# Attention followed by a mixer MLP: one more block of the first channel product computed with seven small products, and its order of issue written anew

## The chip, the cores and the metric

The kernel runs on one core of one Trainium2 chip. The time is device microseconds of that core for one execution; of the kernel before it is the median of three runs. A profile of one execution, with each engine's instructions in order of time, goes with it.

## What is computed

Inputs are q, k, v (4 batches, 8 heads, 768 rows, 64 columns), 16 centroids per head and four weights. First an attention whose mask lets a query see the keys of its own cluster; the heads side by side give x. Then a mixer on x, all in float32:

```python
# x: (4, 768, 512), from attention
h = np.maximum(x.transpose(0, 2, 1) @ w_tok1, 0.0) @ w_tok2      # 768 -> 256 -> 768, over tokens
u = x + h.transpose(0, 2, 1)
h2 = np.maximum(u @ w_ch1, 0.0) @ w_ch2                          # 512 -> 1536 -> 512, over channels
return (u + h2).astype(np.float32)
```

## The kernel before

**Stages.** Attention goes through 16 pairs of heads (to about 316 us of the profile). Then the token products of batches 0, 1 and 2, 3 (`tok1`, `tok2_chunks`), which add h onto x, so that x becomes u. Then the channel products, batch by batch in the order 0, 2, 3, 1. Each batch has three parts: a part computes 512 of the 1536 hidden columns (`ch1_pair`, the first channel product, with relu) and multiplies them at once with their rows of the second weight (`ch2_chunks`), adding onto x. Twelve parts in all, some 35 us each. After a batch's third part its rows go out.

**Seven products.** A product of two matrices that are cut into 2 x 2 blocks is computed with seven block products in place of eight (Winograd's form): left sums S1 to S4, right sums T1 to T4, and seven products, called by `SEVEN` (L551) `p1` A11 B11, `p5` S1 T1, `c11` A12 B21, `u2` S2 T2, `c12` S4 B22, `c22` S3 T3, `c21` A22 T4. `by_turns` (L746) goes through the 21 chunk products of a second-channel stage in the order p1, p5, c11, u2, c12, c22, c12, c11, c21 and lets VectorE add each bank of PSUM onto x.

The first channel product is such a product too, with 128-column chunks i = 0, 1. In the first part of the first batch all seven are plain (`ch1_plain`, L831). In the other eleven parts (`ch1_sets`, L864) four of the seven block products are themselves computed with seven small ones of 192 columns: Y = A12 B21, P = S1 T1, Z = S4 B22, X = A22 T4. The three others, A11 B11, S2 T2 and S3 T3, are big products of 384 columns, two halves for each chunk. The small ones' own sums of weights are in `w1ss` (`set_lefts`, L602), those of u in `uTss` (`set_rights`, L620).

The results gather in SBUF: a11, p5, c12, a22, a12 (each two chunks of 384 columns). ScalarE copies or relus, VectorE adds a bank of PSUM onto them. a11, c12, a22 and a12 after their relu, and the sums S1 to S4 made of them, are the left side of the second-channel stage.

**Order of the work.** The kernel is issued by hand: each engine runs its instructions in the order of the calls in the program, and waits on semaphores for what they read or overwrite. Three lists hold work to be put between products:

- `late`: what of the first channel product is issued behind the start of the second-channel stage. `between` (L740) takes one entry from it each time. `by_turns` calls it after each chunk product, behind the hook `after[m]` of that step (L765 to L767). Before, `late_1` and `late_2` (L945, L950) are taken after steps 0 and 1.
- `others`: sums of weights and of u for the next stages, on VectorE. One is taken at each `between`.
- `turning`: the transposes of u of the next batch (`u_steps`, L713). `u_take` (L693) copies a block of x into `urows` on ScalarE and issues a DMA transpose into `ucols`; `u_put` (L706) copies `ucols` into uT on ScalarE. Three `u_take` go into the first channel product of a batch's third part (`beside`), the rest, eight `u_put` and five `u_take`, are issued by the hook `after[3]` of the second-channel stage.

In the third part `after[15]` and `after[17]` begin the sums of the next batch's u; the rest are issued between the two batches and through `others`.

**Memory.** x of batch 1 is written to a DRAM tile after the first pair's token products and read back when batch 0 is out, into batch 0's place (L1157, L1215).

Of the kernel before, what the change touches and what calls it, by code (L numbers as in the profile page):

```python
# [18 lines left out]
C = 16  # L19
# [31 lines left out]
def kernel(  # L51
# [49 lines left out]
    tokpool = pool("tokpool", 1, tokens)  # L101
    staging = fast.enter_context(ExitStack())
# [30 lines left out]
    spill = spilled.tile([P, NJ, DM], F32, name="spill")  # L133
    xs = [(x1pool if b == 1 else xpool).tile([P, NJ, DM], F32, name=f"x{b}") for b in range(B)]
# [466 lines left out]

    def set_lefts():  # L602
        if "l2" not in pools:
            pools["l2"] = pools["w2sums"].tile([P, 4, 3, HS], F32, name="w1ss")
        l2 = pools["l2"]
        yx = W["ch1"].rearrange("p f (i r c) -> p f i r c", i=2, r=2)[:, 2:4]
        pz = pools["w1s"][:, 0:3:2].rearrange("p i f (r c) -> p f i r c", r=2)
        for n, both in enumerate((yx, pz)):
            blocks = [both[:, f, :, r] for r in range(2) for f in range(2)]
            sums_ = [l2[:, 2 * n : 2 * n + 2, m] for m in range(3)]  # L610
            yield dict(
                zip(("A11", "A12", "A21", "A22", "S1", "S2", "S4", "S3"), blocks + sums_ + blocks[2:3])
            )
# [6 lines left out]
    def set_rights():  # L620
        uT, R, r2 = pools["uT"], pools["R"], pools["r2"]
        yz = uT[:, :, 2:4].rearrange("p n f (k t) -> p n f k t", k=2)
        x, p = (R[name].rearrange("p f (k t) -> p f k t", k=2) for name in ("T4", "T1"))
        for blocks, sums_ in (
            ([yz[:, :, f, k] for f in range(2) for k in range(2)], [r2[:, 0:2, m] for m in range(3)]),
            ([x[:, f, k] for f in range(2) for k in range(2)], [r2[:, 2, m] for m in range(3)]),
            ([p[:, f, k] for f in range(2) for k in range(2)], [r2[:, 3, m] for m in range(3)]),
        ):
            yield dict(
                zip(("B11", "B12", "B21", "B22", "T1", "T2", "T4", "T3"), blocks + sums_ + blocks[1:2])  # L630
            )

    def set_right_sums():

        pools["r2"] = pools["w2sums"].tile([P, 4, 3, HS // 2], F32, name="uTss")
        return [list(winograd_right(blocks)) for blocks in set_rights()]

    def set_blocks():

        (yx, pz), (yz, x, p) = (list(y) for y in (set_lefts(), set_rights()))  # L640
        left = {name: {k: a[:, i] for k, a in two.items()} for two, i, name in
                ((yx, 0, "Y"), (yx, 1, "X"), (pz, 0, "P"), (pz, 1, "Z"))}
        right = {"Y": {k: b[:, 0] for k, b in yz.items()}, "Z": {k: b[:, 1] for k, b in yz.items()},
                 "X": x, "P": p}
        return left, right
# [100 lines left out]
    def by_turns(n, product, of, last=False, after=()):  # L746
# [10 lines left out]
        for m in range(len(order) // 2):  # L757
# [9 lines left out]
            between()  # L767
# [16 lines left out]
    def ch1_pair(part, sets, beside):  # L784
# [6 lines left out]
        p5, c12 = (pools["mlp"].tile([P, 2, HS], F32, name=k) for k in ("p5", "c12"))  # L791
# [10 lines left out]

        def big(psum, a, r, i, start):
            product(psum, a, r, i, start)
            between()
            if a != "A11" and beside:
                beside.pop(0)()
# [13 lines left out]
        def sums_34():  # L821
            nc.vector.scalar_tensor_tensor(
                out=h2["S3"], in0=c12, scalar=0.0, in1=a11, op0=ALU.max, op1=ALU.subtract
            )
            sub(h2["S4"], a12, h2["S2"])

        (ch1_sets if sets else ch1_plain)(
            part, product, big, relu, a11, a12, a22, p5, c12, sum_1, sum_2, sums_34
        )

    def ch1_plain(part, product, big, relu, a11, a12, a22, p5, c12, sum_1, sum_2, sums_34):  # L831
# [24 lines left out]
        def late_(i):  # L856
            product(X[i], "A22", "T4", i, False)
            nc.scalar.activation(out=a12[:, i], in_=X[i], func=ACT.Relu)
            (sums_34 if i else sum_2)()
# [4 lines left out]
    def ch1_sets(part, product, big, relu, a11, a12, a22, p5, c12, sum_1, sum_2, sums_34):  # L864

        left, right = set_blocks()
        n0, n1 = slice(0, HS // 2), slice(HS // 2, HS)

# [7 lines left out]
        def direct(bank, which, start=True):  # L876
            small(bank[:, n0], which, "c11", start)
            small(bank[:, n1], which, "c12", start)

        def chain(q, which, name, x):  # L880

            small(q[:, n0], which, name, name == "p1")
            src = q[:, n0]
            if len(x.shape) == 3:
                src = src.unsqueeze(1).to_broadcast([P, 2, HS // 2])
            add(x, src, x)

        def column(z, which, x):
            small(z[:, n0], which, "p5")
            add(x[:, :, n1], z[:, n0].unsqueeze(1).to_broadcast([P, 2, HS // 2]), x[:, :, n1])  # L890

        X = [ptile("X", HS), None]
        big(X[0], "A11", "B11", 0, True)
        nc.scalar.copy(out=a11[:, 0], in_=X[0])  # L894
        ybe = ptile("Y", HS)
        direct(ybe, "Y")
        add(a11[:, 0], ybe, a11[:, 0])
        X[1] = ptile("X", HS)
        big(X[1], "A11", "B11", 1, True)
        nc.scalar.copy(out=a11[:, 1], in_=X[1])  # L900
        pbe = ptile("Z", HS)
        direct(pbe, "P")
        nc.scalar.copy(out=p5[:, 0], in_=pbe)
        yq, pq = ptile("Y", HS), ptile("Z", HS)
        chain(yq, "Y", "p1", a11[:, 0, n0])
        chain(pq, "P", "p1", p5[:, 0, n0])
        big(X[0], "S2", "T2", 0, False)
        chain(yq, "Y", "u2", a11[:, 0, n1])
        yz, pz = ptile("X", HS), ptile("Z", HS)
        column(yz, "Y", a11)  # L910
        chain(pq, "P", "u2", p5[:, 0, n1])
        small(pz[:, n0], "P", "p5")
        nc.scalar.copy(out=p5[:, 1, n1], in_=pz[:, n0])
        relu(a11[:, 0])
        add(p5[:, 0, n1], pz[:, n0], p5[:, 0, n1])
        add(c12[:, 0], X[0], p5[:, 0])
        big(X[1], "S2", "T2", 1, False)
        chain(yq, "Y", "c22", a11[:, 1, n1])
        chain(pq, "P", "c22", p5[:, 1, n1])
        direct(ybe, "Z")  # L920
        chain(yq, "Y", "c21", a11[:, 1, n0])
        small(pq[:, n0], "P", "c21", False)
        nc.scalar.copy(out=p5[:, 1, n0], in_=pq[:, n0])
        relu(a11[:, 1])
        add(c12[:, 0], ybe, c12[:, 0])
        chain(yz, "Z", "p1", c12[:, 0, n0])
        add(c12[:, 1], X[1], p5[:, 1])
        big(X[0], "S3", "T3", 0, False)
        add(a22[:, 0], X[0], p5[:, 0])
        relu(a22[:, 0])  # L930
        chain(yz, "Z", "u2", c12[:, 0, n1])
        column(pbe, "Z", c12)
        big(X[1], "S3", "T3", 1, False)
        add(a22[:, 1], X[1], p5[:, 1])
        relu(a22[:, 1])
        chain(yz, "Z", "c22", c12[:, 1, n1])
        direct(X[0], "X", False)
        nc.scalar.copy(out=a12[:, 0], in_=X[0])
        small(X[1][:, n0], "X", "c21", False)
        nc.scalar.copy(out=a12[:, 1], in_=X[1])  # L940
        chain(yz, "Z", "c21", c12[:, 1, n0])
        chain(yq, "X", "p1", a12[:, 0, n0])
        sum_1()

        def late_1():  # L945
            chain(yq, "X", "u2", a12[:, 0, n1])
            column(pz, "X", a12)
            sum_2()

        def late_2():  # L950
            chain(yq, "X", "c22", a12[:, 1].rearrange("p (k t) -> p k t", k=2))
            relu(a12)
            sums_34()

        late.extend([late_1, late_2])
# [166 lines left out]
    for b in (0, 2):  # L1122
# [26 lines left out]
        if b == 2:  # L1149
            take(turning, len(turning))  # L1150
            usums = u_sums()
            tok2_chunks(b, {13: lambda: next(usums)})
        else:
# [3 lines left out]
            nc.sync.dma_start(spill, xs[1])  # L1157
# [7 lines left out]
    batches = (0, 2, 3, 1)  # L1165
    for n, b in enumerate(batches):
        turning = []
        for part in range(3):
# [8 lines left out]
            ch1_pair(part, not first, [turning.pop(0) for _ in turning[:UCOLS]])  # L1177
# [25 lines left out]
            if part == 2 and not last:  # L1203

                yz, x, p = steps
                yz[0]()
                yz[1]()
                next(usums)

                others += [lambda: next(usums)] * 2  # L1210
                others.append(lambda: [step() for step in (yz[2], p[2], yz[3], p[3])])
                others += [lambda: None, lambda: (x[0](), x[1]()), lambda: (x[2](), x[3]())]
                if n == 0:
                    xs[1] = xpool.tile([P, NJ, DM], F32, name="x0")
                    nc.sync.dma_start(xs[1], spill)  # L1215
# [216 lines left out]
```

## Time and profile before

| | us |
|---|---|
| median of 3 runs | 823.48 (823.17 to 823.51) |
| the profiled execution | 823.35 |
| its span, first to last instruction | 821.6 |
| TensorE matmul busy | 814.2, 4348 instructions |
| VectorE busy | 631.1, 1206 instructions |
| ScalarE busy | 374.7, 573 instructions |
| one channel part, 535.7 to 570.7: TensorE, VectorE, ScalarE busy | 35.0, 21.7, 5.6 |

A profile page gives for each engine its busy time (PE is TensorE's matmuls, PEld its weight loads, DVE VectorE, ACT ScalarE, POOL GpSimd, SP the engine that issues DMAs). A line of the order of time reads: start in us, duration in us, engine, line of the program, operation, tile written <- tiles read, shapes, count; in square brackets how long the engine was idle before, and what released it. A float32 product appears as two matmul instructions on TensorE. Instructions overlap a little: the duration of one runs on past the start of the next, so the step from start to start is what a queue of them costs.

The rows of a table of stretches read: stretch, length, busy time and count of PE, PEld, DVE, ACT and POOL, mean granted TensorE clock, DMA share, GB/s.

### The profile page before, as it was taken

What the parts mean: (1) busy time and instruction counts of PE and PEld (TensorE: products, weight loads), DVE (VectorE), ACT (ScalarE), POOL (GpSimd) and SP (SyncE); (2) the same over time, 40 slices, a digit from 0 to 9 for tenths busy, and PEclk for the clock granted to TensorE, in tenths of its full rate; (3) what the DMA queues carried; (4) which work ended last, traced back from release to release, by engine and by line L of the source; (5) the groups of instructions that cost most, each with busy time, mean ns of one, the idle gap of its engine ahead of it and who ended that gap; (6) DMA issues with size and microseconds to landing.
All of it is one profiled execution on the core that took longest, in us unless ns stands there. A gap on an engine that the chain in (4) does not pass through costs nothing.

```text
span 821.6 us, 11693 instructions
## 1 busy us (share of the span) xinstructions
PE 814.2 (99%) x4348; PEld 535.5 (65%) x4348; DVE 631.1 (77%) x1206; ACT 374.7 (46%) x573; POOL 30.7 (4%) x28
## 2 busy tenths in 40 slices
PE   8999999999999999999999999999999999999997
PEld 4444444444444444444588888888888888888876
DVE  6879898989898978859797788755777566775665
ACT  5588776777878776127202154121441204511120
POOL 1001010111011000000000000000000000000000
PEclk9999999999999999999999999999999999999999
DMA  8797666768676434143000025000240001400002
GB/s 156 142 162 135 140 142 122 149 139 163 130 160 137 95 104 122 51 127 79 0 1 1 5 45 183 1 0 1 38 117 0 1 1 30 125 1 1 1 0 81
DMA packets 184258, 63.41 MB, mean 77 GB/s; under 512 B 172800, under 2 KB 176896, under 8 KB 183936
## 3 DMA queue, kind: packets, MB, share of 16 engines
q1 hardware_dynamic: 182592, 62.18, 34.7%
q8 instruction: 36, 0.59, 0.3%
q10 hardware_dynamic: 1600, 0.39, 0.2%
q14 instruction: 30, 0.25, 0.1%
HBM read 36.21 MB, written 7.86 MB: 54 GB/s over the span
## 4 chain that ended last, share of the span: by engine, by line
PE 98%; DVE 1%; issue 0%; ACT 0%; DVEq 0%; ACTq 0%
PE sc L413 19%; PE av L455 15%; PE pX L966 15%; PE pX L798 12%; PE pZ L966 7%; PE ph L534 5%; PE pY L871 5%; PE pZ L871 4%; PE pX L871 4%; PE pY L966 4%; PE pX L774 3%; PE small L491 2%; PE pZ L774 1%; PE small L304 1%; PE pZ L798 1%; PE pY L774 1%
## 5 line engine op out<-in xcount | busy, mean ns | idle before, releaser
L437 ACT ACTIVATE ex<-sc 128x768 f32<-128x768 f32 x192 | 151.0, 812 | 27.2 <-PE sc L413 15.5
L413 PE MATMUL sc<-qkT 64*128 64x384 f32 x768 | 155.3, 483 | 0.0
L445 DVE TENSOR_TENSOR sum<-sum,ex 128x768 f32<-128x768 f32 x128 | 127.8, 999 | 27.1 <-ACT ex L437 14.9
L455 PE MATMUL av<-ex,va 128*64 128x384 f32 x768 | 127.4, 488 | 0.0
L566 DVE TENSOR_TENSOR x<-pX,x 128x256 f32<-128x256 f32 (+1 forms) x168 | 75.8, 458 | 38.1 <-PE pX L966 37.6
L455 PEld LDWEIGHTS av<-ex,va 128*64 128x64 f32 x768 | 53.7, 137 | 71.7 <-issue 67.6
L413 PEld LDWEIGHTS sc<-qkT 64*128 64x128 f32 x768 | 67.8, 187 | 38.3 <-issue 38.0
L810 ACT ACTIVATE hA<-hA 128x384 f32<-128x384 f32 (+1 forms) x57 | 34.0, 597 | 85.4 <-DVE hA L566 85.1
L566 DVE TENSOR_TENSOR hA<-pY,hA 128x192 f32<-128x192 f32 (+1 forms) x90 | 36.7, 407 | 45.4 <-PE pY L871 42.7
L798 PE MATMUL pX<-uT,wc 128*128 128x384 f32 x192 | 69.8, 487 | 0.0
L894 ACT COPY hA<-pX 128x384 f32<-128x384 f32 x11 | 5.3, 479 | 131.3 <-PE pX L798 131.3
L413 PE MATMUL sc<-ohT 64*128 64x384 bf16 x384 | 62.4, 323 | 0.0
L462 ACT COPY avrows<-av 128x768 uint16<-128x768 uint16 x32 | 25.5, 797 | 44.4 <-PE av L455 44.4
L566 DVE TENSOR_TENSOR x<-pZ,x 128x256 f32<-128x256 f32 (+1 forms) x84 | 36.4, 455 | 11.4 <-PE pZ L966 11.3
L798 PEld LDWEIGHTS pX<-uT,wc 128*128 128x128 f32 x192 | 35.4, 190 | 14.7 <-issue 0.6
L534 PE MATMUL ph<-x,wt 128*128 128x512 f32 x96 | 41.6, 593 | 0.0
L413 PEld LDWEIGHTS <-ohT 64*128 64x128 bf16 x384 | 18.7, 94 | 33.8 <-issue 9.6
L966 PE MATMUL pX<-wc,hA 128*128 128x256 f32 x144 | 36.9, 380 | 0.3 <-ACT hA L940 0.3
L711 ACT COPY uT<-ucols 128x768 uint16<-128x768 uint16 x32 | 33.2, 1049 | 4.7 <-DMA ucols<-urows 4.7
L966 PE MATMUL pZ<-wc,hS 128*128 128x256 f32 x144 | 35.0, 379 | 0.0
L966 PE MATMUL pY<-wc,hA 128*128 128x256 f32 x144 | 35.0, 379 | 0.0
L798 PE MATMUL pX<-uTs,w1s 128*128 128x384 f32 x96 | 34.9, 486 | 0.0
(189 smaller groups left out, 1310.8 us busy)
## 6 DMA issues: line engine op xcount, KB each, us to landing
raw<-in_moe_w_ch_dram SPq DMA_DIRECT2D x24, 512.0 KB, 4.5
va<-in_v_dram SPq DMA_DIRECT2D x16, 384.0 KB, 3.7
out_dram<-x SPq DMA_DIRECT2D x24, 256.0 KB, 2.3
qk<-in_k_dram SPq DMA_DIRECT2D x60, 96.0 KB, 4.0
qk<-in_q_dram SPq DMA_DIRECT2D x60, 96.0 KB, 3.5
raw<-in_moe_w_tok_dram SPq DMA_DIRECT2D x3, 512.0 KB, 4.1
raw<-in_moe_w_tok_dram SPq DMA_DIRECT2D x4, 384.0 KB, 3.8
spill<-x SPq DMA_DIRECT2D x1, 1536.0 KB, 5.1
```

Of the source, the lines that this page charges most:

```text
L413: nc.tensor.matmul(sc[:, h, 0:HS], lhsT=src[rows, 1, j], rhs=src[rows, 0, HJ * qh : HJ * qh + HJ], start=start, stop=not start,)
L437: nc.scalar.activation(out=ex, in_=sc[:, :, 0:HS], func=ACT.Exp, scale=SM_SCALE)
L445: nc.vector.tensor_tensor(out=acc, in0=acc if j > 1 else st["ex", qh, 0], in1=st["ex", qh, j], op=ALU.add)
L455: nc.tensor.matmul(av[h * D : (h + 1) * D], lhsT=st["va"][:, h, j], rhs=ex[:, h], start=(j == 0), stop=(j == NJ - 1),)
L534: nc.tensor.matmul(pf, lhsT=W["tok1"][:, j, t * P : (t + 1) * P], rhs=xs[b][:, j], start=(j == 0), stop=(j == NJ - 1),)
L566: nc.vector.tensor_tensor(out=dst, in0=a, in1=b, op=ALU.add)
L711: nc.scalar.copy(out=out, in_=pools.pop(("ucols", i)).rearrange("p w j t -> p w (j t)"))
L774: nc.tensor.matmul(psum, lhsT=A[a][:, i], rhs=R[r], start=start, stop=True, skip_group_check=not start,)
L798: nc.tensor.matmul(psum, lhsT=A[a][:, k, c], rhs=R[r][:, k], start=start and k == 0, stop=k == 1, skip_group_check=not start,)
L810: nc.scalar.activation(out=x, in_=x, func=ACT.Relu)
L871: nc.tensor.matmul(psum, lhsT=left[which][a][:, part * P : part * P + P], rhs=right[which][r], start=start, stop=True, skip_group_check=no ...
L966: nc.tensor.matmul(psum, lhsT=h2[a][:, k, i * P : (i + 1) * P], rhs=Bw[w][:, part + 3 * k], start=start and k == 0, stop=k == 1, skip_grou ...
```

## The change

S3 T3 becomes a fifth block product, U, made of seven small ones in the eleven parts, with a result u3 of its own in SBUF. a22 and a12 are then put together on VectorE: V (bank X plus p5) is added onto c12 (C), then u3 is added to a22 (B); E is bank X plus u3 into a12.

The calls of `ch1_sets` are replaced by a list of names, `CH1`. An operation's name is a letter for the block (Y, P, U, Z, X) and one for the product (a, d, f, g, z, be); `+` is VectorE's addition of that bank, `c` ScalarE's copy; `s1` to `s4` are the sums of the second-channel stage, `r11`, `r22`, `r12` the relus, `aside` one `u_take`. Names such as yz0, x1, u2, T3 are sums of u for a new batch, issued only in its first part (`extra`), now from this list and not between the batches. All eight banks are taken at the head, by the table `BANKS`. What follows the first bar of the list is put into `late`, a piece for each bar, so it is taken after steps 0 to 6 of the second-channel stage.

`between` in `by_turns` now takes as many of `others` as spread them evenly over the steps that are left. x of batch 3 is written to DRAM too, after the second pair's token products, in a tile of its own; batches 3 and 1 are read back when batches 0 and 2 are out. The hooks `after[3]`, `after[15]` and `after[17]` are as before.

```diff
+    x3pool = pool("x3pool", 1, tokens)
-    xs = [(x1pool if b == 1 else xpool).tile([P, NJ, DM], F32, name=f"x{b}") for b in range(B)]
+    spill = {b: spilled.tile([P, NJ, DM], F32, name=f"spill{b}") for b in (1, 3)}
+    homes = (xpool, x1pool, xpool, x3pool)
+    xs = [homes[b].tile([P, NJ, DM], F32, name=f"x{b}") for b in range(B)]
...
-        for n, both in enumerate((yx, pz)):
+        for n, both in ((slice(0, 2), w1[:, 2:4]), (slice(2, 4), pz), (slice(4, 5), w1[:, 0:2, 1:2])):
...
+            ([u[:, f, k] for f in range(2) for k in range(2)], [r2[:, 4, m] for m in range(3)]),
...
             if m in after:
                 after[m]()
-            between()
+            between(-(-len(others) // max(len(order) // 2 - m, 1)))
...
+    CH1 = """
+        p1_0 yz0 T2 Zz T3 a11_0 p1_1 Zcz yz1 p2 Ube u0 a11_1 u1 p3 Za u2 Uc0 Pbe u3 T4 Pa Pc0 Ya Ua
+        yz2 Zbe +Pa +Ya Pd +Ua Zc0 aside yz3 u2_0 +Pd +Za x0 x1 Ud x2 Pz x3 Zd +Zz Pcz Pf +Ud Uz +Pz
+        V0 u2_1 Ucz aside +Zd +Pf +Uz C0 Zf Yd B0 Yz +Zf Pg r22_0 +Yd Uf +Yz Pcg Zg +Uf Yf V1 Zcg
+        Ybe +Yf Ug C1 Yg +Ybe Ucg Xbe +Yg r11_0 B1 Xa Xg r11_1 E0 Xz r22_1 aside +Xa
+        |
+        E1 s1 Xd
+        |
+        +Xd s2
+        |
+        Xf +Xz
+        |
+        +Xf
+        |
+        r12 s3
+        |
+        
+        |
+        s4
+    """
...
+        bank = [ptile(tag, HS) for tag in "XXXZZZYY"]
...
+            do[f"V{i}"] = lambda: add(a22[:, i], X[i], p5[:, i])
+            do[f"C{i}"] = lambda: grow(c12[:, i], a22[:, i])
+            do[f"B{i}"] = lambda: grow(a22[:, i], u3[:, i])
+            do[f"E{i}"] = lambda: add(a12[:, i], X[i], u3[:, i])
...
+        first, *rest = CH1.split("|")
+        issue(first)
+        late.extend([lambda names=names: issue(names) for names in rest])
...
-        def late_1():
-            chain(yq, "X", "u2", a12[:, 0, n1])
-            column(pz, "X", a12)
-            sum_2()
-
-        def late_2():
-            chain(yq, "X", "c22", a12[:, 1].rearrange("p (k t) -> p k t", k=2))
-            relu(a12)
-            sums_34()
-
-        late.extend([late_1, late_2])
...
+            nc.sync.dma_start(spill[3], xs[3])
...
-                if n == 0:
-                    xs[1] = xpool.tile([P, NJ, DM], F32, name="x0")
-                    nc.sync.dma_start(xs[1], spill)
+                for name, sums_ in zip(("yz", "x", "p", "u"), steps):
+                    for m, step in enumerate(sums_):
+                        if name != "p" or m > 1:
+                            extra[f"{name}{m}"] = step
+                for m in (2, 3, 4):
+                    extra[f"T{m}"] = lambda: next(usums)
+                if n < 2:
+                    later = batches[n + 2]
+                    xs[later] = xpool.tile([P, NJ, DM], F32, name=f"x{b}")
+                    nc.sync.dma_start(xs[later], spill[later])
```

The call of the hook, which the change leaves as it was, in the loop over parts (L1187 to L1189 of the kernel before):

```python
            after = {}
            if part == 2 and not last:
                after[3] = lambda: take(turning, len(turning))
```

## The prediction

> **What bounds the kernel now.** I read the engine totals first, then the chain of work that ended last, then the order of time in one part of the channel stage.
>
> ```profile
> PE 814.2 (99%) x4348; PEld 535.5 (65%) x4348; DVE 631.1 (77%) x1206; ACT 374.7 (46%) x573; POOL 30.7 (4%) x28
> ...
> PE 98%; DVE 1%; issue 0%; ACT 0%; DVEq 0%; ACTq 0%
> ```
>
> TensorE (PE) is busy from end to end and is 98% of the chain. So PE time saved is time saved, and every wait of PE is paid in full. In the second half I compared each matmul's start with the one before: they follow one another at a fixed step, and the waits I find add up to about 2.3 us (0.3 at each of three changes of batch, 0.8 in the first batch's second part, 0.6 near the end). The steps: 0.1625 us for 192 columns, 0.3225 for 384, 0.216 for 256. Each float32 product is two such instructions, so a product costs 0.325, 0.645 and 0.432 us.
>
> **What is removed and added on PE.** The order of issue of both kernels, counted: 44 products of 384 columns go (S3 T3, two chunks, two halves, in 11 of the 12 parts), 77 of 192 columns come (seven in each). 44 x 0.645 = 28.4 us less, 77 x 0.325 = 25.0 more: **3.4 us saved**, 0.31 a part. That is the whole gain there is to have.
>
> **The largest cost: one relu behind thirteen copies.** The last piece of a12 and its relu (`r12`) are issued later than before. Before, `late_2` (with the relu) ran after the second product of the second-channel stage. Now the rest of the list is cut into seven pieces, one after each product, and `r12` is in the fifth. But in part 2 of each batch but the last, the hook `after[3]` issues, after the fourth product, all that is left of the transposes of the next batch: eight copies into uT (`u_put`) and five out of x (`u_take`), on ScalarE (ACT). So on ACT's queue `r12` now stands behind thirteen copies, in three of the parts. The first `c11` product reads a12 and waits for `r12`, and all of PE stands behind it. Before:
>
> ```profile
> 480.93 0.48 ACT L940 COPY hA<-pX 128x384 f32<-128x384 f32 x1
> 486.18 0.84 ACT L810 ACTIVATE hA<-hA 128x768 f32<-128x768 f32 x1 [4.76 <-DVE hA L566]
> 486.93 1.04 ACT L711 COPY uT<-ucols 128x768 uint16<-128x768 uint16 x1
> 487.84 0.82 ACT L698 COPY urows<-x 128x768 uint16<-128x768 uint16 x1
> ...
> 498.86 1.05 ACT L711 COPY uT<-ucols 128x768 uint16<-128x768 uint16 x1 [0.92 <-DMA ucols<-urows]
> ```
>
> The second line is `r12` in the old place, then come the thirteen copies: from 486.93 to 499.91, 12.98 us, some of it waits for transposes (median 2.8 us from issue to landing). The 4.76 us idle ahead of the relu also show that ACT doesn't pass a waiting instruction, though copies with landed data stood behind it.
>
> [...]
>
> Now the place in time, with 0 where the first product of the second-channel stage starts. On ACT the list ends `r11_0 r11_1 r22_1 aside`. `+Yg` releases the first of these; the product Yg is followed by five products of 192 columns (1.6 us), so `+Yg` starts at -1.4 (0.2 us after its product's step ends, as in all rows) and ends at -1.1. The relus of 384 columns follow at 0.4 each, the third `aside` copy starts at about -0.1, the first uT copy at 0.6, and 13.0 us later the last is done, at 13.6. As the third transpose now is only just issued, one later copy waits a little: 0.1 to 0.2. `r12` then takes 0.84, to 14.6. `c11` would have started at six products of 432 ns and two of 325: 5.83. **Stall 8.8 us, three times: 26.3 us.** If the copies started 0.5 earlier it is 8.3, with more waits for transposes 9.5.
>
> **A smaller cost in the other eight parts: VectorE (DVE) is late.** The new list gives DVE three operations more between the first products (E1 and s1 come behind the first x addition). DVE's steps, from these rows:
>
> ```profile
> 518.00 0.42 DVE L566 TENSOR_TENSOR x<-pX,x 128x256 f32<-128x256 f32 x1
> 518.33 0.35 DVE L566 TENSOR_TENSOR hA<-pY,hA 128x192 f32<-128x192 f32 x1
> 518.81 0.56 DVE L566 TENSOR_TENSOR hA<-pZ,hA 128x384 f32<-128x384 f32 x1
> 519.28 0.95 DVE L563 TENSOR_TENSOR hS<-hS,hA 128x768 f32<-128x768 f32 x1
> 520.15 0.42 DVE L566 TENSOR_TENSOR x<-pX,x 128x256 f32<-128x256 f32 x1
> 520.48 0.55 DVE L566 TENSOR_TENSOR hA<-pY,hA 128x384 f32<-128x384 f32 x1
> ```
>
> Start to start: 0.33 for 256 columns, 0.47 for 384, 0.87 for 768; 0.28 for 192 in other rows. Walked through: first x addition 1.06 (product ends 0.86), E1 1.39, s1 1.86, second addition 2.73, `+Xd` 3.06 to 3.41. PE could start Xf at 2.91, but Xf adds onto the bank that `+Xd` reads: it starts at 3.46, **0.55 late**. Further: s2 3.34, third addition 4.21, `+Xz` 4.54, the first p5 addition 5.01, `+Xf` 5.34 to 5.89, `r12` 5.93 to 6.78. PE has done Xf and three p5 products by 6.37 and waits until 6.83: **0.46**. Together 1.0 a part, 8 parts: 8.1 us. Bounds 0.5 and 1.5 a part, as a step of 0.1 in five DVE operations shifts both. The second part of the first batch also has four additions of 512 columns (some 0.6 each) among these pieces, one ahead of each: 1.8 more (0 to 2.5), in place of the 0.8 it loses now.
>
> **Start of a new batch (three parts).** Ahead of `+Pa` DVE issues yz0 to yz2, T2 to T4, two sums of p, four of u: 3 x 0.47 + 3 x 0.87 + 6 x 0.28 = 5.7 us, from 0.6 after the part starts (the last x addition), so `+Pa` ends at 6.7. Pd, onto the same bank, would start at 6.15. With later small waits 0.9 a part, 0.3 now: **1.8 more**. Bounds 0 and 3.
>
> **What an idle PE costs after it.** At the span's start and end:
>
> ```profile
> 1.23 3.70 PE L1032 MATMUL av<-warm 128*128 128x384 bf16 x11 [1.23 <-DVE warm L1019]
> ...
> 16.25 0.33 PE L413 MATMUL sc<-ohT 64*128 64x384 bf16 x2
> ...
> 818.00:821.60 3.60, 0.00 (x0) 0.00 (x0) 0.00 (x0) 0.00 (x0) 0.00 (x0) 0.96 0.27 94
> ```
>
> The first eleven matmuls step at 0.32 us (the next work starts at 4.73), the same shape later at 0.16: after idling PE ran at half speed, for some 4.2 us. The granted clock of 0.96 after the last matmul (817) says that the half clock came back 0.3 us before the end at 821.6, about 4 us into idling. A stall of 8.8 us is twice that, so I expect half speed for about 4.2 us behind each: 2.1 lost, three times **6.4 us**. No stall of this length is in the trace; ends 0 and 2.6 each.
>
> [...]
>
> **Edits costed at nothing.** 44 ACT copies: ACT is busy 5.6 of 35 us in an ordinary part; if that cover went, some 1.3 us a part. x of batch 3 to memory at about 394: the old spill landed 5.1 us after issue; set sums first write where it lay some eleven big products (14 us) later. Without that cover 5 us, once. Its reload is issued at the end of batch 0, 70 us ahead of its first reader, against 7.0 us to landing. Sixteen sums of U (128 and 192 columns) in the first batch go into DVE's free time or are counted above.
>
> **Sum** against the profiled run's own 823.35 us (span 821.6; the median of the runs, 823.48, is 0.13 above): 823.35 - 3.4 + 26.3 + 8.1 + 1.0 (1.8 less the 0.8 lost now) + 1.8 + 6.4 = **863.5 us**.
>
> **Rivals.**
> - *The clock stays up.* Same stalls, no half speed: 857.1. For it: the trace shows only idling at the ends. Against it: 8.8 us is twice the idling that lowered the clock.
> - *The copies don't hold `r12`.* If they were done sooner or the relu stood elsewhere, the three parts would cost 1.0 as the others: 823.35 - 3.4 + 11 x 1.0 + 1.0 + 1.8 = 833.8. For it: ACT has the room on average. Against it: the order of issue on ACT has eight uT copies directly ahead of the relu.
> - *Only the gain is left* (faster): PE never waits in the new places, 819.9. One mechanism: a12 finished in time. Place: `r12` ahead of `c11`. Price: 3.4 us won. It decides when `+Xd` ends by 2.9 and `r12` by 5.8 after the first product starts; the walk has 3.4 and 6.8, and 14.6 in three parts. That the change wouldn't do its seven products is excluded by the count.
>
> **Chances.** Forecast 0.65, clock stays up 0.20, copies don't hold 0.11, only the gain 0.04. Under 0.2% can't be told from no change here. Faster 0.03 and same 0.01 come from the last case; slower 0.96. The range holds the first two. Low: -3.4 + 3 x 8.3 + 8 x 0.5 + 0 + 0 - 0.8 = +24.7, 848. High: -3.4 + 3 x 9.5 + 8 x 1.5 + 2.5 - 0.8 + 3 + 7.8 = +49.6, 873; with part of the spill's 5 us 875.
>
> **What would show it.** In the profile after: `c11` waiting for the 768-column relu about 8.8 us three times, directly behind a uT copy, and half-step matmuls after it; under the PE waits Xf for `+Xd` 0.5 and `c11` 0.5 in other parts; PE busy down to some 95%. It is wrong if ACT's relu comes before the copies, if PE's idle is far from 35 us, or if matmuls after the long waits keep their step.

## The result, and the profile after

The changed kernel takes 868.44 us (median of 6 runs, 867.30 to 869.66) against 823.30 us (822.85 to 823.51): a ratio of 1.055, interval 1.0536 to 1.0563. The forecast was 863.5 us, with 848 to 875 as its range.

The totals and the chain of the changed kernel:

```profile
PE 826.9 (95%) x4414; PEld 545.4 (63%) x4414; DVE 653.4 (75%) x1300; ACT 388.1 (45%) x617; POOL 30.7 (4%) x28
...
PE 87%; DVE 6%; ACT 3%; DMA 3%; issue 1%; ACTq 0%; DVEq 0%
```

PE is no longer the whole chain. 12% of it is now ACT, DVE and the transposes (the DMA in this row), work that had been hidden. PE's busy time rose although it has less to do: some of its instructions ran at half clock, and two small products behind a wait are busy for 0.59 us in place of 0.49. Without the three long waits shown below it is 820.5 (the first experiment), and 809.9 without nearly all others (the last order below, 819.41 us).

The groups of waits, one line each (engine, tile and line, what was waited for: us in total, times, the longest):

```profile
PE pY L997 <- ACT hA L818: 25.9, 11, 8.0
```

That is `c11` waiting for the relu `r12`: eleven times, 25.9 us, up to 8.0 each. Before, this pair is not among the sixty largest waits. One third part on ACT, in order of time:

```profile
602.17 0.81 ACT L702 COPY urows<-x 128x768 uint16<-128x768 uint16 x1
602.89 1.05 ACT L715 COPY uT<-ucols 128x768 uint16<-128x768 uint16 x1
...
614.85 1.04 ACT L715 COPY uT<-ucols 128x768 uint16<-128x768 uint16 x1 [0.65 <-DMA ucols<-urows]
615.76 0.83 ACT L818 ACTIVATE hA<-hA 128x768 f32<-128x768 f32 x1
```

The relu comes last, behind the thirteen copies that followed it before. And on PE in the same part:

```profile
605.96 2.75 PE L997 MATMUL pZ<-w2s,hS 128*128 128x256 f32 x12
616.65 3.78 PE L997 MATMUL pY<-wc,hA 128*128 128x256 f32 x8 [7.93 <-ACT hA L818]
```

Eight instructions take 3.78 us behind this wait; in an ordinary part (at 655.73) the same eight take 1.99. Granted clock in three stretches, one within the wait and two behind it (the clock is the third figure from the end):

```profile
610.00:611.00 1.00, 0.00 (x0) 0.00 (x0) 0.00 (x0) 1.00 (x2) 0.00 (x0) 0.94 0.60 112
616.60:620.40 3.80, 3.75 (x9) 3.04 (x10) 1.29 (x2) 0.00 (x0) 0.00 (x0) 0.50 0.00 0
621.00:622.00 1.00, 1.00 (x6) 0.82 (x5) 0.27 (x1) 0.00 (x0) 0.00 (x0) 0.94 0.00 0
```

0.94 over 1 us means half clock for 0.12 of it: it fell at 610.88, 2.2 us after PE ran dry at 608.71. The 0.94 of the last row puts its return at 621.12, 4.5 us after PE had resumed.

Where the 45.2 us between the two spans (821.6 and 866.8) came from, by the start of each part's first product:

| parts | before | after | more, in all |
|---|---|---|---|
| third parts of batches 0, 2, 3 | 35.08, 34.97, 34.97 | 45.30, 45.90, 46.28 | 32.5 |
| first parts of batches 2, 3, 1 | 35.28, 35.41, 35.28 | 36.88, 36.90, 36.89 | 4.7 |
| second parts of batches 2, 3, 1 | 34.97 each | 35.94, 35.93, 35.93 | 2.9 |
| second part of batch 0 | 35.58 | 37.95 | 2.4 |
| last part and tail | 40.3 | 43.0 | 2.6 |
| everything ahead of these | 429.75 | 429.92 | 0.2 |

### The profile page after: what moved, and what is told of

It reads as the page before. It is cut to its first block, busy times and chain, and to the rows that moved or that the text cites. A ratio compares the mean times of both kernels' runs of the same rounds, so it can differ in the third digit from the quotient of the medians.

```text
span 866.8 us, 11949 instructions
## 1 busy us (share of the span) xinstructions
PE 826.9 (95%) x4414; PEld 545.4 (63%) x4414; DVE 653.4 (75%) x1300; ACT 388.1 (45%) x617; POOL 30.7 (4%) x28
## 4 chain that ended last, share of the span: by engine, by line
PE 87%; DVE 6%; ACT 3%; DMA 3%; issue 1%; ACTq 0%; DVEq 0%
PE sc L415 18%; PE av L457 15%; PE pX L997 12%; PE pX L802 8%; PE pZ L920 7%; PE ph L536 5%; PE pY L997 5%; PE pZ L997 4%; PE pY L920 4%; DMA ucols<-urows 3%; PE pX L778 2%; DVE hA L568 2%; PE pX L920 2%; ACT hA L818 1%; PE small L493 1%; DVE x L568 1%
## 5 line engine op out<-in xcount | busy, mean ns | idle before, releaser
L962 ACT COPY hA<-pX 128x384 f32<-128x384 f32 x22 | 10.5, 478 | 179.8 <-PE pX L802 179.8
L818 ACT ACTIVATE hA<-hA 128x384 f32<-128x384 f32 (+1 forms) x57 | 31.5, 589 | 77.7 <-DVE hA L568 77.7
L997 PE MATMUL pY<-wc,hA 128*128 128x256 f32 x144 | 41.2, 428 | 25.9 <-ACT hA L818 25.9
L997 PEld LDWEIGHTS pY<-wc,hA 128*128 128x128 f32 x144 | 29.7, 213 | 34.6 <-ACT hA L818 30.3
L568 DVE TENSOR_TENSOR p<-pZ,p 128x192 f32<-128x192 f32 x44 | 15.6, 354 | 41.7 <-ACT p L948 34.7
L568 DVE TENSOR_TENSOR x<-pY,x 128x256 f32<-128x256 f32 (+1 forms) x42 | 19.1, 459 | 34.0 <-PE pY L997 33.5
L802 PE MATMUL pX<-uT,wc 128*128 128x384 f32 x104 | 37.7, 487 | 0.0
```

The costliest lines, as they stand in the source:

```text
L568: nc.vector.tensor_tensor(out=dst, in0=a, in1=b, op=ALU.add)
L802: nc.tensor.matmul(psum, lhsT=A[a][:, k, c], rhs=R[r][:, k], start=start and k == 0, stop=k == 1, skip_group_check=not start,)
L818: nc.scalar.activation(out=x, in_=x, func=ACT.Relu)
L997: nc.tensor.matmul(psum, lhsT=h2[a][:, k, i * P : (i + 1) * P], rhs=Bw[w][:, part + 3 * k], start=start and k == 0, stop=k == 1, skip_grou ...
```

## The experiments

Theory 1 is the forecast's: the cost is one of order, above all `r12` behind the copies. Theory 2 puts it down to the additional work: VectorE and ScalarE too full for the fifth set, or the transposes slowed by it.

**The hook two steps later.**

```diff
-                after[3] = lambda: take(turning, len(turning))
+                after[5] = lambda: take(turning, len(turning))
```

> The changed kernel with the hook of the remaining transposes two steps later (step 5, behind the piece with r12), so that r12 stands ahead of the thirteen copies on ScalarE. Theory 1 (r12's place behind the copies costs the three third parts 10.3, 10.9 and 11.3 us over the kernel before, clock included): these parts become as the ordinary ones (+1.0 each), so 868.4 - 32.6 + 2.9 = 838.7 us, between 836 and 842. Theory 2 (the third parts are long because the transposes and copies themselves now take too long beside the additional copies and additions): c11 or a later reader of uT waits on, and the time stays above 855.

Measured: 837.90 us, ratio 1.0179 (1.0162 to 1.0196). The third parts fell to 37.03, 35.93 and 35.92. The last two are as long as an ordinary part; in the one of batch 0, three sums of weights from `others` stand on DVE between the additions ahead of `c11`, which starts 1.0 later. On ACT the relu stands first again:

```profile
490.68 0.84 ACT L818 ACTIVATE hA<-hA 128x768 f32<-128x768 f32 x1 [5.99 <-DVE hA L568]
491.43 1.04 ACT L715 COPY uT<-ucols 128x768 uint16<-128x768 uint16 x1
```

The same work in another order takes 30.5 us less. Theory 2 doesn't explain the third parts.

**TensorE kept busy during the wait.** 24 additional products (results not used) ahead of the waiting `c11`:

```diff
+                def fill():
+                    psum = ptile("Y", HS)
+                    for _ in range(24):
+                        nc.tensor.matmul(
+                            psum[:, 0:192], lhsT=ident,
+                            rhs=rcps.rearrange("p n i h j -> p (n i h j)"), start=True, stop=True,
+                        )
+
+                after[5] = fill
```

> The changed kernel with 24 additional float32 products of 192 columns (7.8 us, results not used) issued on TensorE just ahead of the waiting c11 in the three third parts, so that TensorE is busy while ScalarE copies. The wait of some 8 us stays, less than 0.5 us of the filling reaches past it. Theory 1 with the clock (TensorE idles long enough to come back at half speed): the slow steps behind the waits (1.1, 2.1 and 2.2 us in the trace) go, 868.4 - 5.4 = 863 us, within 861.5 to 865. Rival (the steps behind the waits are slow for another reason, such as reloading weights or banks): no change, 867 to 870. If TensorE were the bound there and not ScalarE, it would be some 20 us slower.

Measured: 862.03 us, ratio 1.0471 (1.0453 to 1.0488). With 7.8 us more work in each of three places the kernel is 6.4 us faster. The products behind the first wait, and a stretch of granted clock across the end of the filling:

```profile
490.50 7.96 PE L1228 MATMUL pY<-rcps,ident 128*128 128x192 f32 x48
498.32 1.99 PE L997 MATMUL pY<-wc,hA 128*128 128x256 f32 x8
```

```profile
496.00:500.00 4.00, 4.00 (x24) 3.67 (x23) 0.52 (x2) 1.75 (x2) 0.00 (x0) 1.00 0.01 4
```

The eight instructions take 1.99 again, at full clock. The idling and not the waiting instruction makes the slow steps; and PE had nothing else to do in that time. From the start of `c11` to the end of the part are 13.05 us in all three places, against 14.52, 15.25 and 15.60 in the changed kernel: half speed cost 1.5, 2.2 and 2.5 (the expectation had 1.1, 2.1 and 2.2), 6.2 in all.

**The clash alone, in the kernel before.** One edit to it, nothing of the fifth set:

```diff
-                after[3] = lambda: take(turning, len(turning))
+                after[1] = lambda: take(turning, len(turning))
```

> The kernel BEFORE with one edit: the hook of the remaining transposes at step 1 in place of 3, which puts the thirteen copies ahead of late_2 with its relu of a12. Nothing of the fifth set is in it. Theory 1: the copies start about 0.4 us after the first product of the stage, last 13.0, the relu ends at 14.3, c11 would start at 6.5: 7.8 us of wait and some 1.8 of slow clock, three times: 823.3 + 29 = 852, between 846 and 856. Theory 2 (the cost comes from the additional products, additions and copies of the change): no more than 3 us above 823.3.

Measured: 855.10 us, ratio 1.0386 (1.0369 to 1.0403).

```profile
494.69 3.78 PE L966 MATMUL pY<-wc,hA 128*128 128x256 f32 x8 [7.45 <-ACT hA L810]
498.27 2.00 PE L966 MATMUL pX<-w2s,hS 128*128 128x256 f32 x5
```

The same wait and the same half speed, in a kernel with four sets. 32 us in place of the 29 expected: the third of the waits was 9.1 where the first two were 7.5 and 7.4, and half speed cost 2.2 to 2.8 a time (by PE's steps, 2.5, 2.8 and 2.2).

**The second spill alone, in the kernel before.**

```diff
...
+            nc.sync.dma_start(spill[3], xs[3])
...
-                if n == 0:
-                    xs[1] = xpool.tile([P, NJ, DM], F32, name="x0")
-                    nc.sync.dma_start(xs[1], spill)
+                if n < 2:
+                    later = batches[n + 2]
+                    xs[later] = xpool.tile([P, NJ, DM], F32, name=f"x{b}")
+                    nc.sync.dma_start(xs[later], spill[later])
```

> The kernel BEFORE with the second spill alone: x of batch 3 in a tile of its own, written to DRAM after the second pair's token products, batches 3 and 1 read back when 0 and 2 are out. The forecast costed it at nothing: 823.1 us, within 0.2%. If the first writes over the spilled tile wait for its transfer, up to 5 us more; if the read back comes too late for the transposes, up to 7 more.

Measured: 823.00 us, ratio 0.9997 (0.9988 to 1.0006). It costs nothing that can be measured.

**The tail of the list in another order.** The changed kernel with its hook where it was, E1 and s1 ahead of the second-channel stage, `r12` two pieces earlier:

```diff
-        V0 u2_1 Ucz aside +Zd +Pf +Uz C0 Zf Yd B0 Yz +Zf Pg r22_0 +Yd Uf +Yz Pcg Zg +Uf Yf V1 Zcg
-        Ybe +Yf Ug C1 Yg +Ybe Ucg Xbe +Yg r11_0 B1 Xa Xg r11_1 E0 Xz r22_1 aside +Xa
+        V0 u2_1 Ucz aside +Zd +Pf +Uz C0 Zf Yd B0 Yz +Zf Pg r22_0 +Yd Uf +Yz Pcg Zg +Uf Yf Zcg
+        Ybe +Yf V1 Ug C1 Yg +Ybe Ucg Xbe +Yg r11_0 B1 Xa Xg r11_1 E0 Xz r22_1 aside +Xa E1 s1
         |
-        E1 s1 Xd
+        Xd +Xd
         |
-        +Xd s2
+
         |
-        Xf +Xz
+        Xf +Xz +Xf r12
         |
-        +Xf
+        s2
         |
-        r12 s3
+        s3
```

> The changed kernel with the tail of the list in another order: E1 and s1 ahead of the second-channel stage, Xz, Xf's addition and r12 together in the third piece (ahead of the hook), s2, s3, s4 one piece later, +Yf ahead of V1. Theory 1 (r12 behind the copies, and VectorE late by a few operations before Xf and c11): both waits go in all eleven parts; what is left over the ideal 819.9 us is the start of three batches (0.8 each) and the additional sums in the first batch (1.0 to 2.0): 822 to 826 us, 823.5 at the middle, no more than 0.3% from the kernel before. Theory 2 (VectorE and ScalarE are too full for the additional operations, in whatever order): the small waits stay at about 1.3 a part and the time is 835 or more.

Measured: 825.06 us, ratio 1.0025 (1.0015 to 1.0035). 43 us are gone with no operation left out, so the small waits too were order and not load. An ordinary part takes 34.85 now (34.97 before the change). What is left of them in an ordinary part stands at Xd, here in the third part of batch 2:

```profile
588.25 0.36 DVE L568 TENSOR_TENSOR hA<-pY,hA 128x192 f32<-128x192 f32 x1
...
588.67 0.30 PEld L920 LDWEIGHTS pY<-uTss,w1ss 128*128 128x128 f32 x2 [0.32 <-DVE hA L568]
588.67 0.59 PE L920 MATMUL pY<-uTss,w1ss 128*128 128x192 f32 x2
```

The addition (`+Xa`) ends at 588.61, 0.02 us after Xd could have started; Xd starts at 588.67 and its step is 0.43 in place of 0.32.

**Three versions on,** each edit against the version before it. First E0 ahead of B1, and none of `others` while pieces are outstanding, one a step after them:

```diff
-            between(-(-len(others) // max(len(order) // 2 - m, 1)))
+            between(0 if late else 1)
...
-        Ybe +Yf V1 Ug C1 Yg +Ybe Ucg Xbe +Yg r11_0 B1 Xa Xg r11_1 E0 Xz r22_1 aside +Xa E1 s1
+        Ybe +Yf V1 Ug C1 Yg +Ybe Ucg Xbe +Yg r11_0 E0 Xa Xg r11_1 B1 Xz r22_1 aside +Xa E1 s1
```

> The list of e3 with two more edits: E0 ahead of B1, so that +Xa ends 0.2 us earlier, before Xd's weights are to be loaded; and of the additional sums none while pieces of the list are outstanding, one a step behind them (the rest at the end of the part). Theory 1 (what is left in e3 are waits of single operations: 0.19 at Xd in each part, 1.3 in the first batch's second part, 0.3 in its third, 1.0 at each start of a batch, 1.1 in the last part): 825.1 - 11 x 0.19 - 1.0 = 822.0 us, 821 to 823. Theory 2 (VectorE is full, and what is gained at one place is lost at another): 824.5 or more.

Measured: 823.87 us, ratio 1.0013 (1.0004 to 1.0023), outside the 821 to 823 expected. The 0.19 at Xd went in ten of the eleven parts (34.66 for an ordinary one), but the additional sums that were left over now came together between the first two parts of batch 0 (430.2 to 433.5 on DVE), and a product waits there:

```profile
PE pZ L920 <- ACT u L948: 1.9, 1, 1.9
```

That is the gain of one place lost at another, but by this edit and not because VectorE is full, as the last of the three versions shows.

Then four copies and T1, T2 earlier:

```diff
+                after[0] = lambda: take(turning, 4)
                 after[3] = lambda: take(turning, len(turning))
...
-                after[15] = first_sums
-                after[17] = lambda: (steps[2][0](), steps[2][1]())
+                after[14] = first_sums
+                after[16] = lambda: next(usums)
+                after[18] = lambda: (steps[2][0](), steps[2][1]())
...
-                for m in (2, 3, 4):
+                for m in (3, 4):
```

> e5 with four of the remaining copies of the transposes issued earlier (step 0, while ScalarE is idle ahead of r12), and with T1 and T2 of the next batch in steps 14 and 16 of the third part, so that VectorE has 0.87 less ahead of +Pa at the start of a batch. Theory 1: the wait of Pd for +Pa (0.6 each with the reload) and the one behind it go in three parts: 2 to 3 us under e5, 819.5 us, 818.5 to 821, so 0.3 to 0.5% under the kernel before. If four copies ahead of r12 hold it again (3.5 us of copies in 4 us of idle time), c11 waits up to 0.5 more in three parts and it is no better than e5.

Measured: 822.58 us, ratio 0.9996 (0.9987 to 1.0005), outside the 818.5 to 821 expected, though 1.3 under the version before. The first parts of a batch fell by 0.9 in two of three (34.70 us), but `r12` ends 0.3 us late in each third part (35.11 for 34.66): four copies ahead of it are too many, the case that the expectation had named. The wait between the first two parts of batch 0 is still there.

Last, sums spread again in the first part of batch 0 alone, and two copies ahead in place of four:

```diff
-        banks, after = {}, dict(after)
+        banks, after, many = {}, dict(after), len(others) > 22
...
-            between(0 if late else 1)
+            between(0 if late else -(-len(others) // max(len(order) // 2 - m, 1)) if many else 1)
...
-                after[0] = lambda: take(turning, 4)
+                after[0] = lambda: take(turning, 2)
```

Here `many` holds where more than 22 sums are outstanding when the stage begins.

> e6 with two edits: the additional sums of the first batch's first part spread over its steps again (e5 and e6 flush five of them between the first two parts, and a product waits 2.05 us behind that), and two copies of the transposes ahead of r12 in place of four (c11 waits 0.35 us + 0.1 in each third part of e6). Theory 1: both waits go, 822.6 - 2.1 - 1.4 = 819.1 us, 818 to 820.5, 0.4 to 0.6% under the kernel before: the 3.4 us of the fifth set in full, and 0.7 more. If VectorE is simply full in the first batch, the 2 us turn up elsewhere and the time is 821 or more.

Measured: 819.41 us (819.12 to 819.76) against 823.27, ratio **0.9956** (0.9942 to 0.9969). This is below both kernels, and an ordinary part takes 34.66 for 34.97 before: the 0.31 a part of the forecast. Its totals and chain:

```profile
PE 809.9 (99%) x4414; PEld 542.9 (66%) x4414; DVE 651.6 (80%) x1300; ACT 389.4 (48%) x617; POOL 30.6 (4%) x28
...
PE 99%; DVE 1%; ACT 0%; issue 0%; DVEq 0%
```

PE is again nearly all of the chain, with the same 4414 instructions as the changed kernel, the same 1300 operations on DVE and 617 on ACT.

**The three counts loaded last.**

```diff
-            if last:
-                both = fits_load()
...
             ch2_chunks(b, part, last, after)
+            if last:
+                both = fits_load()
```

> e8 with the loading of the three counts into registers behind the last second-channel stage and not ahead of it. In e6 the first product of that stage waits 1.07 us there (0.5 in the kernel before) though the relu named ended earlier, so I put it down to TensorE's own loads. Theory: 1.0 us less than e8, 818 us. Rival: the loads then stand in the tail between the last addition and the output rows on the engine that issues them, and the time is as e8 or up to 2 us more.

Measured: 819.74 us, ratio 0.9959 (0.9945 to 0.9972), no gain over 819.41. The wait is gone: the last part comes to its first second-channel product after 15.89 us and not 16.95, and the last addition onto x starts 0.8 us earlier (812.32 for 813.12). But from there to the end of the span are 5.9 us and not 4.4. That is the time the rival foretold; that the loads make the end longer is not shown, as the changed kernel's profile has 6.1 there with the loads in their old place.

## Why the prediction was right, step by step

**The place of the relu: right, nearly to the digit.** 8.8 us a third part were forecast for the waits at Xf and `c11` together. On PE's steps they measure 8.8, 8.8 and 8.8 (in batch 2, with ordinary step widths taken off: 0.56 at Xf, 0.10 behind it, 8.10 at `c11`). The 5.83 at which `c11` would have started is right, and is what `c11` keeps in the best order, but it is twelve products of 432 ns (six of the 21 chunk products, two each) and two of 325, not six. The walk took the copies' 12.98 us as they stood; in the trace after they run from 602.89 to 615.89, 13.0. The clash alone put into the kernel before, and the hook moved alone, show it from both sides. That all three came out to the digit is in part luck: in the filled kernel one copy waited 1.98 us for its transpose (0.22 in the same place of the changed kernel), and in the clash run the third wait was 1.6 us longer than the other two.

**Half speed behind the waits: right, 6.4 us forecast, 6.2 measured** on the steps behind them. That the two kernels' times differ by 6.4 too is chance: by their profiles, the filled one has 6.2 less there, 1.5 less at the very end and 0.4 less ahead of the parts, but waits 1.7 longer in batch 2, where a transpose came late. One assumption was off, a fixed 4 us into idling and 4.2 us into the next work. The clock at the other two waits:

```profile
494.00:495.00 1.00, 0.00 (x0) 0.00 (x0) 0.00 (x0) 1.00 (x2) 0.00 (x0) 0.91 0.65 121
501.00:502.00 1.00, 1.00 (x5) 0.86 (x4) 1.00 (x3) 0.00 (x0) 0.00 (x0) 0.68 0.00 0
730.00:731.00 1.00, 0.00 (x0) 0.00 (x0) 0.00 (x0) 1.00 (x3) 0.00 (x0) 0.67 0.67 129
740.00:741.00 1.00, 1.00 (x5) 0.84 (x4) 0.16 (x1) 0.00 (x0) 0.00 (x0) 0.71 0.00 0
```

It fell at 494.82, 610.88 and 730.34 (3.8, 2.2 and 2.9 us into the idle times) and came back at 501.64, 621.12 and 740.58 (3.0, 4.5 and 5.2 us after PE had resumed, 4.2 only on average). These times lie on a grid: half clock lasted 6.82, 10.24 and 10.24 us, two and three times 3.41, and the falls are 116.06 and 119.46 apart, 34 and 35 times 3.413. For the clash run there is an estimate from PE's steps, each loss behind a wait taken twice: it puts the returns 116.0 and 116.1 apart, 34 times 3.41 again. So what a stall of this length costs behind it, 1.5 to 2.8 us in these six, goes, by these numbers, with where it lies on the grid. The forecast had 2.1 us for each; the three of the changed kernel cost 1.5, 2.2 and 2.5, 2.1 on average.

**DVE late at Xf and `c11`: right in place, small in size.** The walk had Xf 0.55 and `c11` 0.46 late in an ordinary part. The changed kernel, PE's instructions behind these waits:

```profile
569.60 0.59 PE L920 MATMUL pY<-uTs,wc 128*128 128x192 f32 x2 [0.27 <-DVE hA L568]
570.03 2.75 PE L997 MATMUL pZ<-w2s,hS 128*128 128x256 f32 x12
572.93 0.48 PE L997 MATMUL pY<-wc,hA 128*128 128x256 f32 x1 [0.15 <-ACT hA L818]
```

Xf is 0.56 late and `c11` 0.32. But the walk lacked two things: 0.19 at the end of the first channel product (Yg waits for `+Yf`, which stands behind V1 on DVE; the order that moved V1 removes it), and a charge on each wait: Xf starts at 569.60 and the next product at 570.03, a step of 0.43 in place of 0.325. So 1.3 us a part and not 1.0. That is the mis-sized term: 0.3 in eleven parts, some 3 us of the 5 by which the forecast was low.

**Start of a batch: right,** 0.9 forecast, 0.96 measured beside the 0.19. **Second part of batch 0: right in kind,** 2.8 forecast, 3.1 measured. What it lost before the change was 0.6 (35.58 for 34.97), not the 0.8 that the sum took off.

**The last part** was forecast as any other, and took 2.6 more than before, not 0.7. 1.1 of it are the waits above. From the start of the last addition onto x to the end of the span are 6.1 us for 4.6 before; the other 1.5 lie there. The kernel with the hook moved and the filled one run the same instructions in their last part and have 4.6 there, so the 1.5 is not shown to belong to the change. Its cause stays open.

**The gain: there, and buried.** 3.4 us were forecast. With the waits gone the fifth set is worth that: 3.9 us at the end (819.41 for 823.27), of which some are waits that the kernel before had itself.

**Edits costed at nothing:** the spill alone measured nothing; the additional copies and additions cost nothing that an order could not hide.

The rivals: the clock did not stay up, the copies did hold the relu, and only the gain was left only after the order was made anew again.

## What to carry to other kernels

Where lists of work meet on one engine, look at the order engine by engine and not list by list: the new list was sound by itself, but a hook that nobody had touched put thirteen copies ahead of one relu, and that cost nine times the gain. Where PE is the whole chain, lay out the few instructions on each other engine that its next waits depend on, with steps from start to start; here that gave places and sizes to a few tenths. Here each long PE wait (7.4 to 9.1 us) cost its length and then 1.5 to 2.8 us for half speed behind it, and each short one (0.08 to 0.44) some 0.1 us on top.

## What the runs showed of the hardware that I had not expected

- The float32 products behind three short waits cost about 0.10 us more, though PE was held up for only 0.08 us at Xd, 0.32 at `c11` and 0.44 at Xf. At all three the load of weights and the matmul start together (588.67 in the lines above; 572.93 and 569.60 in the changed kernel); for the product behind Xf, which waits for nothing, the load starts 0.16 earlier (569.87 for a matmul at 570.03).
- TensorE's clock fell to 0.50 as early as 2.2 us after its work ran out, in the middle of the kernel, and stayed there up to 5.2 us into the next work. Its six changes around the waits of the changed kernel lie on one grid of 3.41 us: from fall to return two, three and three steps of it, from fall to fall 34 and 35.
- Idle TensorE time filled with products nobody needs made the kernel 6.4 us faster (868.44 to 862.03).
